# Other banks for one pair of output blocks, later landings for a batch's first loads, and a new instruction order in a fused attention and FFN kernel

## The chip, the cores and the metric

The kernel runs on one core of a Trainium2 chip. The metric is the device time of one execution in microseconds (us); the median of a few executions is compared.

The core's engines run side by side, each through its own list of instructions in a fixed order, and wait for each other by semaphores: PE (TensorE) multiplies matrices, DVE (VectorE) and ACT (ScalarE) work elementwise, POOL (GpSimd) here casts and issues DMAs, and SP (SyncE) issues DMAs. Sixteen DMA engines move the data. PE writes its results to PSUM, which has eight banks; DVE and ACT read them from there.

## The reference

Clustered attention for 4 batches, 8 heads, 768 positions and 64 dimensions, and then a gated FFN over the 3072 positions with 512 features and 1536 hidden units:

```
q_assign = argmax(q_n · c_n)            # 16 centroids per head, normalised; k_assign in the same way
scores   = where(q_assign == k_assign, scale * q·kT, -1e9)
attn     = exp(scores - max) / sum
x        = (attn · v), heads side by side
out      = (sigmoid(x @ w_gate) * (x @ w_val)) @ w_out
```

## The kernel before, in words

**Tiling.** Heads are taken in pairs (`p`, four of them per batch). Positions are split in even and odd halves; a group `(b, gr)` is the half `gr` of batch `b`, 384 positions (in batch 0: 256 and 512). A block is one head pair in one group.

**Attention.** `load_nat` (L444) loads k and q of a head pair into a buffer `nat`. For batch 0 and for the first half of batch 1's pairs, PE transposes them (L617, L795, L903) into a `ring` bank; for the rest DVE does (L595). Copies go to `t32`, POOL casts to `even` (L650), a DMA on SP shifts half of it to `odd` (L654). PE multiplies with the centroids (L687, L835, L948), DVE makes one-hot rows of the best cluster (L549, L556, L563, L574), and DMAs put these rows below the features (L334), so that the score matmul with 80 rows gives the mask as well. `attend` (L983) then does, for two units at a time: two score matmuls into an `sc` buffer (L1008), one exponential on ACT into `es` (L1032), and the value matmuls into the `av` bank (L1059). At the end of a block DVE divides (L1084, L1089), and a transposing DMA on SP (L1117), or PE (L1097), puts the result into `x`.

**FFN.** `feed` (L1409) runs for a group when its attention is done. For a hidden chunk of 128 it makes a gate and a value projection into two `ring` banks (L1422, four matmuls each), a tanh on ACT (L1585), and a product on DVE into `hT` (L1596). Pairs of chunks that stand in `seven` are made with seven instead of eight products (L1498), whose sums go through ACT copies (L1517) and DVE additions (L1529, L1544); in the last group, (3, 1), both of the first banks of these seven products are one `sc` buffer, and elsewhere two `ring` banks. `project` (L1187) multiplies two blocks of 128 positions with w_out, again with seven products (L1275, six matmuls each), sums on DVE (L1244, L1306, L1310, L1327, L1331, L1348) and one ACT copy (L1321). Its argument `many` decides where its results and sums stand: with `many` in two `sc` buffers and in three buffers `late` (batch loads' buffers, free by then), else in two `ring` banks and in buffers `s22`, `s11`, `s12`, `half`, `diff`.

**PSUM.** The eight banks are two `sc` buffers of two banks, one `av` bank and three `ring` banks.

**What sets the order.** No order is written by hand. Each step is added to a list (`od.add`) with an engine, a cost, its dependencies, a due time, a latency `lat` behind its end, and the buffers it takes. `Order.schedule` (L129) goes through a model of time: of the steps that could start first on an engine it takes the one with the smallest due time. What it finds is the order of instructions on each engine; the due times come from `due_at` for attention slots and `due_ffn` for FFN work. So a changed constant moves instructions on all engines, and nothing else. A POOL or SP DMA may wait for an older one of its queue.

Of the kernel before, what the change touches and what calls it, by code (L numbers as in the profile page):

```python
# [209 lines left out]
def kernel(  # L210
# [108 lines left out]
    def due_at(slot):  # L319
        return T1 + (slot - S1) * (0.403 if slot < S1 else 0.826)  # L320

# [122 lines left out]
    def load_nat(b, p, nm, eng, due, early=0.0, hold=None, behind=()):  # L444
# [38 lines left out]
        if hold:  # L483
# [12 lines left out]
                1.05, held, due, acq=[] if held else [buf], uses=[buf] if held else [], early=early,  # L496
                seq=behind, lat=2.0 if b else (0.2 if p == 1 else 1.0),
            )
# [80 lines left out]
    def prepare(b, grp, due, step, act=(), queues=("SP",), split=False):  # L579
# [116 lines left out]
        for half in range(2):  # L696
# [33 lines left out]
            if split or half:  # L730
                n_ = 0
                cs = cols if split else ALL
                for e in range(2):
                    for pos, p in enumerate(grp):
                        for g, nm in ((2 * pos, "k"), (2 * pos + 1, "q")):
                            r = 32 * g + 16 * e
                            m = dma(
                                queues[n_ % len(queues)],
                                lambda p=p, e=e, nm=nm, cs=cs: aug[b, p][e].tile[64:80, NM[nm], cs],
                                lambda r=r, cs=cs: oht.tile[r : r + 16, cs],  # L740
                                0.04 if split else 0.07,

                                [a5, shifted[b, p, half]], due - (20.0 if (b, grp[0]) == (1, 0) else 0),
                                uses=[oht, aug[b, p][e]], lat=3.2,
                            )
                            n_ += 1
                            for h in (half,) if split else (0, 1):
                                masked[b, p, e, nm, h].append(m)
# [30 lines left out]
    def prepare_pair(b, p, due, step, act=("q",), direct=False):  # L779
# [82 lines left out]
        if direct:  # L862
            place(
                b, p, oh, tiles, last, due + (3.0 if p == 1 else 0.0), [c["k", 0], c["k", 1]],
                {(nm, e, h): c[nm, e] for nm in ("k", "q") for e in range(2) for h in range(2)},
            )
            return
# [115 lines left out]
    def attend(block, at, slot):  # L983
# [15 lines left out]
        for i, (e, j) in enumerate(some):  # L999
            kb = aug[b, p][j % 2]  # L1000

            def score(i=i, e=e, j=j, kb=kb):
# [15 lines left out]
                    masked[b, p, j % 2, "k", e] + masked[b, p, par, "q", e],  # L1018
                    due - (33.5 if early else 0.0), lat=0.25,
                    acq=[] if i else [sc], uses=[kb, qb_] + ([sc] if i else []),  # L1020
# [32 lines left out]
        def value():  # L1053
# [14 lines left out]
            value, [t2] + [vload[b, p][e] for e in dict.fromkeys(e for e, _ in some)],  # L1068
            due + (-4.1 if last else 5.5) - (19.5 if early else 0.0), lat=0.25 if last else 0.0,
            seq=exps[-1:], acq=[av] if first else [], uses=[es] + ([] if first else [av]),  # L1070
# [116 lines left out]
    def project(b, one, two, final, many, end):  # L1187
# [45 lines left out]
        def add(to, place, x, y, op, behind=(), on="DVE"):  # L1233
            tasks = []
            on = "DVE" if end else on
            for n, (i0, i1) in enumerate(parts):
# [11 lines left out]
                        (done1 if done1 is not done2 else []) + done2[: 2 * i1] + list(behind)[n : n + 1],  # L1248
                        due - -13.0 - (6.0 if end and not n else 0.0), lat=0.13, acq=fresh, both=True,
                        uses=hs + [buf for buf in to if buf not in fresh],  # L1250
# [158 lines left out]
    def feed(b, gr, work):  # L1409
# [23 lines left out]
        free = [h_last[hs_[-3]]] if len(hs_) > 2 else []  # L1433
        seven = WP[: {(0, 0): 0, (0, 1): 0, (1, 0): 2, (1, 1): 2, (2, 0): 2, (2, 1): 3, (3, 0): 3, (3, 1): 2}[b, gr]]
        if not wsums_of:
            for n, fa in enumerate(WP):
                sum_up_weights(n, fa, 70.0 + 2 * n)
# [11 lines left out]
        if seven:  # L1449
            for n, (to, x, y) in enumerate(  # L1450
# [6 lines left out]
                def differ(to=to, x=x, y=y, n=n):  # L1457
                    if not n:
# [4 lines left out]
                    od.add(  # L1463
                        "DVE", 0.28, differ, xdone[b, gr] + t_tasks[-1:], due_ffn(work) - 6.0, lat=0.12, both=True,
                        acq=[] if n else [tb], uses=[xb] + ([tb] if n else []), seq=free,
# [3 lines left out]
        def seven_products(fa, work):  # L1469
# [39 lines left out]
            def copied(i, r_, m, eng="ACT", y=0):  # L1509
# [3 lines left out]
                def go():  # L1513
# [7 lines left out]
                return od.add(  # L1521
                    eng, 0.375 if eng == "ACT" else 0.47, go, [m], due_ffn(work) - 5.0, lat=0.16,
                    acq=[to] if new else [], uses=[r_] + ([] if new else [to]),
# [93 lines left out]
        if len(blocks_of) % 2:  # L1617
# [3 lines left out]
        pairs = [  # L1621
            project(b, blocks_of[i], blocks_of[i + 1], end and i + 2 == len(blocks_of), (end and i > 0) or (b, gr) == (B - 1, 0), end)
            for i in range(0, len(blocks_of), 2)
# [22 lines left out]
    load_v(0, NP - 1, "SP", -7.7 + p_, 20.0 + 4.5 * NP, behind=nat[0, NP - 2, "v"])  # L1646
    WT = (12.5, 16.0, 23.0, 24.0, 29.5, 29.5, 38.0, 29.0, 43.0)
    n = 0
# [15 lines left out]
    for block in blocks:  # L1664
        b, gr, p, part = block
        if (gr, p) == (0, 0) and b + 1 < B:
            for grp in ((0, 1), (2, 3)):
                due = due_at(first_slot(b + 1, grp[0]))
                for p_ in grp:
                    for nm in ("k", "q"):  # L1670

                        load_nat(
                            b + 1, p_, nm, "POOL" if (b, grp[0]) == (0, 2) else "SP", max(due - 45.0, 20),
                            due - 60 if b else 40.0 if grp[0] else 14.5,
                        )
                prepare(b + 1, grp, max(due - 27.5, 45.5) + (9.0 if (b, grp[0]) == (0, 2) else 0), 1.31)
        at = 0
# [5 lines left out]
        if done[b, gr] == NP * len(groups[b, gr]):  # L1683
            if b + 1 < B:
                for p_ in (2 * gr, 2 * gr + 1):
                    due = due_at(first_slot(b + 1, p_))
                    load_v(b + 1, p_, "POOL", due - 32.0, due - 15, due - 12.5)
            work = feed(b, gr, work)
# [45 lines left out]
```

## Time and profile before

| what | value |
|---|---|
| median of 3 runs | 315.62 us (315.27 to 318.08) |
| the profiled execution's own time | 316.29 us |
| its span, first to last instruction | 314.5 us |
| PE, DVE, ACT, POOL busy | 97%, 75%, 75%, 25% |
| matmuls on PE | 3251 |
| granted TensorE clock, mean | 0.999 |
| HBM read, written | 28.34 MB, 6.29 MB |

How to read it: in the lists of instructions the first number is the start in us from the beginning of the span, then the time taken, the engine, the line of the kernel, the operation, what it writes <- reads, shapes, a count, and in brackets the idle time of the engine before it with what ended that. A matmul's row spans its way through the array, so that rows of matmuls overlap: the cost of one is read from start to start. Rows with SPq or a POOL DMA are the issue of a transfer, not its landing.

### The profile page before, as it was taken

To read this page: it belongs to the slowest core of one execution; us is meant where nothing else is said; L and a number is where in the kernel's file an instruction comes from. 1 tells how busy PE (TensorE), PEld (TensorE's weight loads), DVE (VectorE), ACT (ScalarE), POOL (GpSimd) and SP (SyncE) were. 2 spreads that over 40 slices of the span, in tenths; PEclk is the share of its full clock that TensorE was granted. 3 is DMA by queue.
4 is the path that set the end of the run, shared out by engine and by line. 5 is a ranking of instruction groups with operands and counts; after the bars stand their busy time and mean duration, and the time that the engine had idled before them with its cause. 6 is when DMAs were issued, how large, how long until landed. Compare 5 with 4: busy or idle time off the path is not lost.

```text
span 314.5 us, 8301 instructions
## 1 busy us (share of the span) xinstructions
PE 303.7 (97%) x3251; PEld 223.0 (71%) x3251; DVE 236.5 (75%) x575; ACT 235.0 (75%) x365; POOL 77.5 (25%) x110
## 2 busy tenths in 40 slices
PE   7998899999999999999999999999999999999895
PEld 3677688644578867757776877757777888768674
DVE  4999847799978749885486978977475944786893
ACT  4799899332999979868897768957899778943521
POOL 5897563881011401340002200470000000000000
PEclk9999999999999999999999999999999999999999
DMA  6999999994465886891465683996200022000003
GB/s 216 376 273 150 238 215 121 124 147 68 82 101 105 142 137 176 105 113 40 106 102 88 104 185 94 100 122 59 83 6 15 15 81 79 16 2 36 34 0 133
DMA packets 97430, 34.49 MB, mean 110 GB/s; under 512 B 83136, under 2 KB 93296, under 8 KB 97392
## 3 DMA queue, kind: packets, MB, share of 16 engines
q1 hardware_dynamic: 72048, 24.30, 34.1%
q0 software_dynamic: 24336, 8.65, 27.1%
q10 hardware_dynamic: 1008, 1.02, 0.9%
q8 instruction: 25, 0.41, 0.5%
q14 instruction: 13, 0.11, 0.1%
HBM read 28.34 MB, written 6.29 MB: 110 GB/s over the span
## 4 chain that ended last, share of the span: by engine, by line
PE 83%; ACT 5%; DMA 5%; DVE 5%; issue 1%; DVEq 0%; SPq 0%; ACTq 0%
PE ring L1422 28%; PE sc L1008 17%; PE ring L1275 15%; PE av L1059 9%; PE ring L1498 8%; ACT es L1032 3%; PE sc L687 3%; DMA nat<-in_q_dram 3%; PE sc L1275 2%; DMA out_dram<-out 1%; PE sc L1498 1%; DMA cn<-in_centroids_dram 1%; DVE t L577 1%; DVE even L574 1%; ACT nat L1517 1%
## 5 line engine op out<-in xcount | busy, mean ns | idle before, releaser
L1032 ACT ACTIVATE es<-sc,nbias 128x768 f16<-128x768 f32 (+1 forms) x189 | 168.6, 923 | 18.4 <-PE sc L1008 17.0
L1059 PEld LDWEIGHTS <-es 128*128 128x128 f16 x1152 | 54.9, 97 | 15.0 <-issue 0.2
L1059 PE MATMUL av<-vp,es 128*128 128x65 f16 x1152 | 60.1, 193 | 0.0
L1585 ACT ACTIVATE gt<-ring 128x384 f32<-128x384 f32 (+2 forms) x68 | 34.2, 503 | 33.9 <-PE ring L1422 26.2
L1422 PE MATMUL ring<-x,wv 128*128 128x384 f16 (+2 forms) x272 | 55.3, 325 | 0.1
L1422 PE MATMUL ring<-x,wg 128*128 128x384 f16 (+2 forms) x272 | 55.4, 326 | 0.0
L1596 DVE SCALAR_TENSOR_TENSOR hT<-gt,ring 128x384 f16<-128x384 f32 (+2 forms) x68 | 37.2, 548 | 21.7 <-PE ring L1422 18.1
L650 POOL CAST even<-t 128x768 f16<-128x768 f32 x24 | 20.5, 871 | 118.8 <-DVE t L595 59.7
L1422 PEld LDWEIGHTS <-wv 128*128 128x128 f16 x272 | 25.0, 97 | 15.8 <-issue 0.8
L1422 PEld LDWEIGHTS <-wg 128*128 128x128 f16 x272 | 24.6, 98 | 15.9 <-issue 2.5
L1275 PEld LDWEIGHTS <-hT 128*128 128x128 f16 x294 | 27.1, 98 | 4.6
L1008 PE MATMUL sc<-even 80*128 80x384 f16 (+2 forms) x120 | 26.3, 293 | 1.7 <-ACT es L1032 1.2
L1008 PE MATMUL sc<-odd,even 80*128 80x384 f16 x96 | 26.3, 326 | 0.4 <-ACT es L1032 0.4
L1008 PE MATMUL sc<-odd 80*128 80x384 f16 x96 | 26.4, 325 | 0.1
L1008 PE MATMUL sc<-even,odd 80*128 80x384 f16 (+2 forms) x120 | 26.4, 293 | 0.1
L1008 PEld LDWEIGHTS <-even 80*128 80x128 f16 x216 | 19.9, 98 | 7.5 <-issue 1.6
L1008 PEld LDWEIGHTS <-odd 80*128 80x128 f16 x216 | 19.5, 98 | 7.6 <-issue 2.9
L1529 DVE TENSOR_TENSOR nat<-ring,nat 128x384 f32<-128x384 f32 x26 | 13.9, 551 | 10.1 <-ACT nat L1517 8.6
L1498 PEld LDWEIGHTS <-wss 128*128 128x128 f16 x224 | 19.0, 97 | 3.5 <-issue 1.9
L595 DVE STREAM_TRANSPOSE t<-nat 128x384 f32<-128x384 f32 x40 | 21.4, 556 | 0.0
L334 POOL DMA_DIRECT2D vp<-in_v_dram x24 | 19.7, 833 | 0.1
L1089 DVE TENSOR_TENSOR xn<-av,rr 128x384 f16<-128x384 f32 (+2 forms) x36 | 18.2, 506 | 0.8
(140 smaller groups left out, 456.3 us busy)
## 6 DMA issues: line engine op xcount, KB each, us to landing
out_dram<-out SPq DMA_DIRECT2D x21, 256.0 KB, 2.4
nat<-in_k_dram SPq DMA_DIRECT2D x32, 96.0 KB, 3.0
nat<-in_q_dram SPq DMA_DIRECT2D x32, 96.0 KB, 3.0
odd<-even SPq DMA_DIRECT2D x12, 192.0 KB, 3.2
vp<-in_v_dram POOLq DMA_DIRECT2D x24, 96.0 KB, 4.8
nat<-in_k_dram SPq DMA_DIRECT2D x5, 384.0 KB, 6.9
nat<-in_q_dram SPq DMA_DIRECT2D x5, 384.0 KB, 7.2
nat<-in_v_dram SPq DMA_DIRECT2D x4, 384.0 KB, 6.9
```

Source lines behind the costliest of these rows:

```text
L334: eng, (0.74 if eng == "POOL" else 0.69) if pkt == 13 else ISSUE[eng], lambda: Q[eng].dma_start(out=out_of(), in_=in_of()),
L595: nc.vector.transpose(t[:, half * QB : (half + 1) * QB].rearrange("p (c x) -> p c x", x=128), blocks_[:, half],)
L650: nc.gpsimd.tensor_copy(t[:, NM[nm], cols], t32[p, nm].tile[:, cols])
L1008: nc.tensor.matmul(out=to, lhsT=kb.tile[0:80, 0, e * QB + j // 2 * 128 : e * QB + (j // 2 + 1) * 128], rhs=qb_.tile[0:80, 1, e * QB + c0 * ...
L1032: i = nc.scalar.activation(to, of, AF.Exp, bias=nbias, scale=D ** -0.5 if quarters(b, p) else scale,).ins
L1059: nc.tensor.matmul(out=av.tile[:, g : g + D + 1], lhsT=es.tile[:, i * N + c * 128 : i * N + (c + 1) * 128], rhs=vp[:, e, j, :], start=firs ...
L1089: nc.vector.tensor_tensor(take(xn)[:, :nq].rearrange("p c (e d) -> p (c e) d", d=D), sums()[:, :, 0:D], rr.tile[:, : 2 * nq].unsqueeze(2). ...
L1275: nc.tensor.matmul(out=ps[:, lo:hi], lhsT=left_()[:, i], rhs=right(i)[:, n0 : n0 + w], start=new and i == 0, stop=i == NFC // 2 - 1, skip_ ...
L1422: nc.tensor.matmul(out=ps[:, :N], lhsT=ws[fc // FPG][:, dcc, fc % FPG, :], rhs=xb.tile[:, dcc, :N], start=(dcc == 0), stop=(dcc == NDC - 1),)
L1498: nc.tensor.matmul(out=ps[:, f], lhsT=w_[:, d, f], rhs=x_()[:, d], start=new and not (f or d), stop=d == 1, skip_group_check=True,)
L1585: lambda rg=rg, gt=gt: nc.scalar.activation(take(gt)[:, :N], rg.tile[:, :N], AF.Tanh, scale=0.5),
L1596: nc.vector.scalar_tensor_tensor(t[:, fc, :N], gt.tile[:, :N], 1.0, rv.tile[:, :N], ALU.add, ALU.mult)
```

## The change

The last pair of group (3, 0) no longer asks for `many`; `seven` of the last group is written out as chunk pairs 2 and 4 (the dictionary gave the first two of `WP`, which are 2 and 4); the planner's latency for loads of whole `nat` buffers of later batches (in effect those of the first two head pairs of batch 1) goes from 2.0 to 3.0; and constants of due times, early times and latencies are set anew. `WT` holds the due times of the weights' loads in order of issue. Nothing else in the code differs.

```diff
     def due_at(slot):
-        return T1 + (slot - S1) * (0.403 if slot < S1 else 0.826)
+        return T1 + (slot - S1) * (0.386 if slot < S1 else 0.826)
...
# load_nat, a whole buffer
-                seq=behind, lat=2.0 if b else (0.2 if p == 1 else 1.0),
+                seq=behind, lat=3.0 if b else (0.2 if p == 1 else 1.0),
...
# prepare, the DMA of a one-hot row
-                                uses=[oht, aug[b, p][e]], lat=3.2,
+                                uses=[oht, aug[b, p][e]], lat=2.7,
...
# prepare_pair, direct
-                b, p, oh, tiles, last, due + (3.0 if p == 1 else 0.0), [c["k", 0], c["k", 1]],
+                b, p, oh, tiles, last, due + (4.0 if p == 1 else 0.0), [c["k", 0], c["k", 1]],
...
# attend, scores
-                    due - (33.5 if early else 0.0), lat=0.25,
+                    due - (29.5 if early else 0.0), lat=0.25,
...
# attend, values
-            due + (-4.1 if last else 5.5) - (19.5 if early else 0.0), lat=0.25 if last else 0.0,
+            due + (-8.1 if last else 5.5) - (19.5 if early else 0.0), lat=0.25 if last else 0.0,
...
# project, sums of hT
-                        due - -13.0 - (6.0 if end and not n else 0.0), lat=0.13, acq=fresh, both=True,
+                        due - -14.0 - (6.0 if end and not n else 0.0), lat=0.13, acq=fresh, both=True,
...
# feed
         seven = WP[: {(0, 0): 0, (0, 1): 0, (1, 0): 2, (1, 1): 2, (2, 0): 2, (2, 1): 3, (3, 0): 3, (3, 1): 2}[b, gr]]
+        if (b, gr) == (B - 1, 1):
+            seven = (2, 4)
...
-                        "DVE", 0.28, differ, xdone[b, gr] + t_tasks[-1:], due_ffn(work) - 6.0, lat=0.12, both=True,
+                        "DVE", 0.28, differ, xdone[b, gr] + t_tasks[-1:], due_ffn(work) - 5.0, lat=0.12, both=True,
...
-                    eng, 0.375 if eng == "ACT" else 0.47, go, [m], due_ffn(work) - 5.0, lat=0.16,
+                    eng, 0.375 if eng == "ACT" else 0.47, go, [m], due_ffn(work) - 3.0, lat=0.16,
...
-            project(b, blocks_of[i], blocks_of[i + 1], end and i + 2 == len(blocks_of), (end and i > 0) or (b, gr) == (B - 1, 0), end)
+            project(b, blocks_of[i], blocks_of[i + 1], end and i + 2 == len(blocks_of), end and i > 0, end)
...
-    WT = (12.5, 16.0, 23.0, 24.0, 29.5, 29.5, 38.0, 29.0, 43.0)
+    WT = (14.5, 16.0, 23.0, 24.0, 29.5, 29.5, 38.0, 29.0, 42.5)
...
-                            b + 1, p_, nm, "POOL" if (b, grp[0]) == (0, 2) else "SP", max(due - 45.0, 20),
-                            due - 60 if b else 40.0 if grp[0] else 14.5,
+                            b + 1, p_, nm, "POOL" if (b, grp[0]) == (0, 2) else "SP", max(due - 45.5, 20),
+                            due - 60 if b else 37.5 if grp[0] else 14.5,
...
-                prepare(b + 1, grp, max(due - 27.5, 45.5) + (9.0 if (b, grp[0]) == (0, 2) else 0), 1.31)
+                prepare(b + 1, grp, max(due - 27.5, 45.5) + (9.0 if (b, grp[0]) == (0, 2) else 0), 1.37)
...
-                    load_v(b + 1, p_, "POOL", due - 32.0, due - 15, due - 12.5)
+                    load_v(b + 1, p_, "POOL", due - 32.0, due - 15, due - 13.5)
```

## The prediction

> **What bounds the kernel now.** I read the page first (span, busy shares), then the busy time by windows, then the waits of PE, and then the order in time on PE, SP, ACT and DVE around each wait. The shares:
>
> ```profile
> span 314.5 us, 8301 instructions
> PE 303.7 (97%) x3251; PEld 223.0 (71%) x3251; DVE 236.5 (75%) x575; ACT 235.0 (75%) x365; POOL 77.5 (25%) x110
> ```
>
> In the windows the columns are the stretch, its length, and the busy time of PE, PEld, DVE, ACT and POOL, then the clock, the busy share of the DMA engines (over 1 where packets overlap) and GB/s.
>
> ```profile
> 30.00:40.00 10.00, 8.10 (x120) 6.61 (x117) 8.59 (x24) 8.76 (x11) 5.23 (x7) 1.00 1.21 229
> 50.00:270.00 220.00, 219.82 (x2360) 159.68 (x2358) 167.20 (x383) 174.36 (x271) 42.37 (x53) 1.00 0.61 95
> 290.00:300.00 10.00, 9.20 (x75) 6.54 (x74) 7.74 (x19) 5.23 (x13) 0.00 (x0) 1.00 0.15 54
> ```
>
> From 50 to 270 us PE is idle for 0.18 us: nothing can be won there, and any new wait there is paid in full. What can be won lies before 50 us, where ACT is as full as PE, and behind 270 us. The waits of PE name the two places:
>
> ```profile
> PE ring L617 <- DMA nat<-in_q_dram: 1.2, 1, 1.2
> PE sc L1498 <- DVE nat L1529: 0.5, 1, 0.5
> PE sc L1498 <- ACT p L1517: 0.3, 1, 0.3
> ```
>
> The clock is 1.00 in every window, so no term below needs it.
>
> **Part 1: what changes nothing by itself.** `seven = (2, 4)` for the last group equals what the dictionary gave (two of WP = two, four): 0 us. PE issues the same matmuls before and after, and DVE, ACT, POOL and SP the same counts of work. So the change is order and banks, and PE's sum of work stays; the time moves only by idle time of PE that goes or comes.
>
> **Part 2: batch 1's first loads.** The larger `lat` (2.0 to 3.0) makes the planner expect these loads later. In the new order the two transposes of `nat` for k of head pair 0 stand side by side instead of two score groups apart, and the load of q for head pair 1, which takes over their buffer, is issued on SP ahead of two transposing DMAs and one row copy instead of behind them. The old order on PE and SP, and the landing (from the chain that ended last):
>
> ```profile
> 23.98 0.52 PE L617 MATMUL ring<-ident,nat 128*128 128x128 f32 x3
> 33.77 0.49 PE L1008 MATMUL sc<-odd,even 80*128 80x384 f16 x2
> 35.41 0.52 PE L617 MATMUL ring<-ident,nat 128*128 128x128 f32 x3 [1.15 <-DMA nat<-in_q_dram]
> ```
> ```profile
> 19.31 0.61 SPq L334 DMA_DIRECT2D odd<-even  x1
> 23.43 1.20 SPq L1117 DMA_TRANSPOSE x<-xn  x1
> 24.71 0.54 SPq L334 DMA_DIRECT2D odd<-even  x1
> 25.54 1.15 SPq L1117 DMA_TRANSPOSE x<-xn  x1
> 26.79 1.44 SPq L334 DMA_DIRECT2D nat<-in_q_dram  x1
> ```
> ```profile
> 26.79 8.49 DMA nat<-in_q_dram
> ...
> 281.69 1.31 PE sc L1275 x12
> ```
> ```profile
> 36.30 4.52 ACT L1032 ACTIVATE es<-sc,nbias 128x768 f16<-128x768 f32 x5 [1.10 <-PE sc L1008]
> ```
>
> The buffer is free by 24.50 in the old order (the second transpose starts at 23.98 and takes 0.52), but SP reaches the load only at 26.79: 2.3 us are lost to the queue. In the new order the buffer is free about 1.5 to 2 us sooner, I estimate at 22.5, and nothing stands before the load on SP behind the row copy of 19.31. With the same 8.49 us it lands at 31.0; PE comes to it at 34.10 (33.77 and two matmuls of 0.16). Even issued only at 24.5 it would land at 33.0. So the wait goes. PE lost 35.41 - 34.10 = 1.31 us by starts, but ACT, which paces this stretch, was idle 1.10 us for it (the row of 36.30): I take 1.1. Bounds: 0, if the load lands as late as before, and 1.3. What comes after it is next late is ACT itself, full from 36.30 on.
>
> What is moved behind the load on SP: two transposing DMAs and a row copy, each 1.44 us later at most by the load's issue. The projections that read them stand behind the transposes of 35.41 in PE's order: cost 0 by that cover, and if it were gone, at most the 1.4 us. POOL issues the first gate weights three casts later; they are read behind the same place: 0.
>
> [...]
>
> **Part 3: the tail.** The pair of blocks of group (3, 0) that is multiplied with w_out beside the start of group (3, 1)'s FFN took both `sc` banks; now it takes two of the three `ring` banks, and the `s22`, `s11`, `s12`, `half`, `diff` buffers. The seven products of (3, 1) live in `sc` and had to wait until the pair was read out. The old rows, in order of time:
>
> ```profile
> 280.23 0.81 PE L1422 MATMUL ring<-x,wg 128*128 128x384 f16 x4
> 280.50 0.55 DVE L1596 SCALAR_TENSOR_TENSOR hT<-gt,ring 128x384 f16<-128x384 f32 x1
> 280.88 0.81 PE L1422 MATMUL ring<-x,wv 128*128 128x384 f16 x4
> ...
> 289.31 0.48 ACT L1517 COPY p<-sc 128x384 f32<-128x384 f32 x1
> ...
> 290.50 0.49 PE L1498 MATMUL sc<-x,wg 128*128 128x192 f16 x4
> ...
> 290.83 0.49 PE L1498 MATMUL sc<-nat,wss 128*128 128x192 f16 x4
> ...
> 291.22 0.56 DVE L1529 TENSOR_TENSOR nat<-sc,nat 128x384 f32<-128x384 f32 x1 [1.21 <-ACT nat L1517]
> 291.83 0.49 PE L1498 MATMUL sc<-nat,wss 128*128 128x192 f16 x4 [0.50 <-DVE nat L1529]
> ...
> 301.58 0.60 PE L1275 MATMUL ring<-wo,hT 128*128 128x256 f16 x4
> ```
>
> By starts, a projection (P, 4 matmuls) takes 0.65 (280.23 to 280.88), a seven-product step (Q) 0.33 (290.50 to 290.83), a w_out product (J, 6 matmuls) 0.65 (1.31 for twelve in the chain's row of 281.69, quoted above). From 280.23 to the first product of the last pairs at 301.58, 21.35 us, the order holds 16 P, 14 Q and 7 J: 10.4 + 4.6 + 4.6 = 19.6 us. So 1.75 us are waits. One is seen whole: 290.83 to 291.83 is 1.00 us for a Q of 0.33. They come from one chain: both sevens can begin only behind the old pair, then run through ACT and DVE with little else between.
>
> In the new order the first Q stands behind four P, the seven J of the pair lie between the steps of the first seven, and the second seven follows. I went through it by hand from 280.23 with the rows' durations: a reader starts 0.27 us behind the start of the next group (280.23 to 280.50), a DVE instruction takes 0.55, an ACT copy 0.48, PE restarts 0.05 behind them (291.78 to 291.83). First Q 282.83; J 283.16 to 285.13; two Q; four J 285.78 to 288.40; four Q to 289.72; then PE waits about 0.4, since DVE must first do the pair's two mixes and last sum and then the Q's own sum: next Q at 290.15; from there P and Q alternate without a wait, and the last P ends at 300.25. That is 1.33 us before 301.58: I take -1.3. Bounds: -1.75, all waits gone, and +0.5, if the single free ring bank makes as many half-us waits as it removes and one more; -1.3 is nearer the first since every other step found its bank free.
>
> Cover of this: six of the ring uses in that stretch are J on the two held banks; P, which needs all three, stands before and behind. If the held banks were read later than about 289.5, the P behind would wait for them one to one.
>
> **Part 4: the rest of the order.** Score and sum due times move by up to 4 us; the row copies of the one-hots are expected 0.5 us sooner (`lat` 3.2 to 2.7). Inside 50 to 270 us the new order differs by neighbours that change place. Cost 0, with PE's 0.18 us of idle time as the row; bounds 0 and +0.5, one wait like the largest of the tail. The last block of w_out's first third (`wo0`) moves on POOL from ahead of batch 1's later loads to behind them, beside its last third; its sums, four DVE instructions, move later, into a stretch in which DVE is full:
>
> ```profile
> 60.00:80.00 20.00, 20.00 (x113) 9.26 (x112) 19.29 (x43) 7.44 (x13) 9.17 (x12) 1.00 0.89 113
> ```
>
> In exchange three others move out behind it, so I take 0 for the difference of one.
>
> **The sum.** -1.1 - 1.3 + 0 = -2.4 us. The profiled execution took 316.29 us (span 314.5 and 1.8 around it): 313.9 for such a one. The median shown, 315.62, is 0.67 below it, so I predict 313.2 against that median.
>
> **The rivals.**
> (a) The load does not land sooner, since the DMA engines are full: the wait at 35.41 stays, and only the tail is won: 314.3. For it: the share of 1.21. Against: loads of this kind and size land a like time behind their issue, 7.2 us in the median of five, so landing follows issue:
>
> ```profile
> nat<-in_q_dram SPq DMA_DIRECT2D x5, 384.0 KB, 7.2
> ```
>
> Chance 0.10.
> (b) The tail's gain is eaten, since the pair holds two of three ring banks: 314.5, the first term alone. For it: three banks fed P without a wait, one can't. Against: the hand count. The Trainium skill (Perfetto Trace Analysis, "Optimization Strategy") says that a gap repeating on the engine that should be full can mean too little PSUM for the next tile; by it this rival is what a shared bank gives. Chance 0.12.
> (c) Slower. DVE's in-order wait for batch 1's last q quarters: POOL now issues `wo0` and the last third back to back ahead of them.
>
> ```profile
> 72.69 1.03 DVE L595 STREAM_TRANSPOSE t<-nat 128x384 f32<-128x384 f32 x2
> ```
> ```profile
> 62.07 3.09 POOL L334 DMA_DIRECT2D nat<-in_q_dram  x4 [1.36 <-DVE t L595]
> ```
> ```profile
> wo<-in_moe_w_out_dram POOLq DMA_DIRECT2D x3, 512.0 KB, 10.6
> nat<-in_q_dram POOLq DMA_DIRECT2D x8, 96.0 KB, 4.4
> ```
>
> Behind this DVE row stand the reads that free ring banks, so PE stops some 1.7 us (one P pair at 512 columns, an estimate from 0.65 per 384) after DVE does. The fourth quarter is issued at about 64.4 and lands 4.4 us later, at 68.8; DVE comes to it at 72.69, or 71.6 with the first term won. If `wo0` adds its whole 10.6 us, it lands at 79.4, DVE is 7.8 us late, PE 6.1: 315.62 - 2.4 + 6.1 = 319.3. Up to 2.8 us of delay it costs nothing, from 6.9 on the kernel is slower than before. Against: the loads ahead of them start sooner by what `wo0` took before, so the queue as a whole is not longer. Chance 0.08.
> (d) It does nothing that counts, both terms given back by new waits in between: 315.6. Chance 0.06.
> (e) More goes: all 1.75 in the tail, 1.3 early, and 0.4 of the other 0.75 us that PE is idle from 30 to 40 us: 312.2. Chance 0.09.
>
> **How the numbers follow.** The forecast has 0.55, with its own range 312.3 to 314.2 (half of each term's doubt). 1% is 3.2 us, about what a measurement of this kernel can tell from no change: faster by over 1% is below 312.46, held by (e) and the lower edge of the forecast: 0.18. Slower by over 1% is above 318.8: (c) at its full price, 0.07. The rest, 0.75, is within 1%. The range 311.8 to 316.2 leaves out (c), and parts of (e).
>
> **What would show it.** Right: the PE wait on in_q_dram at L617 is gone; ACT's idle 1.10 us near 36 is gone; the first run of L687 (batch 1's second half) starts 1.1 us sooner; the first L1498 on `sc` of the last group stands about 3 us behind its first L1422, and the waits of L1498 shrink from 0.8 to about 0.4; the last products start 1.3 us sooner after the first P. Wrong: PE waits at L1422 behind the pair's ring banks near 289 to 292; DVE waits at L595 between 68 and 75; a wait over 0.5 us between 50 and 270. A span above 314 would say that a term failed.

## The result, and the profile after

The changed kernel takes 313.38 us in the median of six runs (312.99 to 313.82), the kernel before 316.36 beside it (315.27 to 318.08): a ratio of 0.9904, 95% interval 0.9884 to 0.9924. That is 3.0 us or 0.96% less. Its profiled execution took 313.21 us, with a span of 311.4 against 314.5: 3.1 us less in the trace, where the prediction had 2.4.

The page of the kernel after; the count of matmuls is that of before (3251) and the busy time of PE the same within 0.1 us (303.8, before 303.7), so all of it is idle time of PE that went:

```profile
span 311.4 us, 8300 instructions
...
PE 303.8 (98%) x3251; PEld 223.1 (72%) x3251; DVE 236.6 (76%) x575; ACT 234.7 (75%) x365; POOL 77.2 (25%) x110
```

Its busy time by windows (columns as in the prediction), and its waits of PE:

```profile
20.00:30.00 10.00, 9.44 (x130) 7.36 (x129) 9.31 (x26) 9.61 (x13) 9.03 (x13) 1.00 1.12 194
30.00:40.00 10.00, 9.50 (x143) 8.22 (x141) 8.85 (x26) 10.00 (x14) 6.76 (x9) 1.00 1.24 209
...
50.00:270.00 220.00, 220.00 (x2363) 159.19 (x2362) 167.55 (x380) 174.29 (x270) 42.21 (x52) 1.00 0.60 97
...
290.00:300.00 10.00, 9.99 (x70) 6.57 (x69) 8.97 (x25) 4.05 (x9) 0.00 (x0) 1.00 0.01 2
```
```profile
PE sc L1008 <- ACT es L1032: 0.9, 2, 0.5
...
PE sc L1500 <- DVE nat L1531: 0.5, 1, 0.5
```

From 30 to 40 us PE is busy for 9.50 us instead of 8.10, from 290 to 300 for 9.99 instead of 9.20, and in the middle for all 220.00 instead of 219.82. The wait for `in_q_dram` at L617 is gone. (From L1437 on, line numbers are two higher than before: L1500 is the old L1498.)

Three places date the gain. The first product of L687, before and after:

```profile
57.85 1.50 PE L687 MATMUL sc<-t,cblk 128*32 128x384 f32 x16
```
```profile
55.85 1.50 PE L687 MATMUL sc<-t,cblk 128*32 128x384 f32 x16
```

The first P (L1422) of the last group starts at 280.23 before, the first product of the last pairs at 301.58; after, they stand here:

```profile
278.01 0.81 PE L1422 MATMUL ring<-x,wg 128*128 128x384 f16 x4
...
280.61 0.49 PE L1500 MATMUL sc<-x,wg 128*128 128x192 f16 x4
280.94 0.82 PE L1275 MATMUL ring<-wo,hT 128*128 128x256 f16 x6
...
287.18 0.49 PE L1500 MATMUL sc<-nat,wss 128*128 128x192 f16 x4
288.17 0.49 PE L1500 MATMUL sc<-nat,wss 128*128 128x192 f16 x4 [0.50 <-DVE nat L1531]
...
298.50 0.82 PE L1275 MATMUL ring<-wo,hT 128*128 128x256 f16 x6
```

So 2.22 us are won ahead of the tail (280.23 to 278.01), 2.00 of them ahead of 58 us, and 0.86 in the tail (a stretch of 21.35 us, now 20.49). The early gain is twice what was predicted, the tail's two thirds.

On SP the load of q is issued at 22.70 us, ahead of two transposing DMAs and a row copy, and lands 5.03 us later:

```profile
19.30 0.61 SPq L334 DMA_DIRECT2D odd<-even  x1
22.70 0.39 SPq L334 DMA_DIRECT2D nat<-in_q_dram  x1
24.27 1.21 SPq L1117 DMA_TRANSPOSE x<-xn  x1
25.57 0.54 SPq L334 DMA_DIRECT2D odd<-even  x1
26.52 3.27 SPq L1117 DMA_TRANSPOSE x<-xn  x2
```

and ACT, idle for 1.10 us at 36.30 before, runs through:

```profile
29.49 8.74 ACT L1032 ACTIVATE es<-sc,nbias 128x1024 f16<-128x1024 f32 x10 [0.32 <-PE sc L1008]
```

### The profile page after: what moved, and what is told of

Same layout as the page of the kernel before. It is cut to its first block, busy times and chain, and to the rows that moved or that the text cites. A ratio compares the mean times of both kernels' runs of the same rounds, so it can differ in the third digit from the quotient of the medians.

```text
span 311.4 us, 8300 instructions
## 1 busy us (share of the span) xinstructions
PE 303.8 (98%) x3251; PEld 223.1 (72%) x3251; DVE 236.6 (76%) x575; ACT 234.7 (75%) x365; POOL 77.2 (25%) x110
## 4 chain that ended last, share of the span: by engine, by line
PE 92%; ACT 4%; DVE 1%; DMA 1%; issue 0%; SPq 0%; ACTq 0%
PE ring L1422 29%; PE sc L1008 19%; PE ring L1275 16%; PE av L1059 11%; PE ring L1500 9%; ACT es L1032 3%; PE sc L687 3%; PE sc L1275 1%; PE sc L1500 1%; DMA nat<-in_k_dram 1%; PE ring L795 1%; PE ring L617 1%; PE ring L835 1%; PE ring L903 0%; PE ring L948 0%
## 5 line engine op out<-in xcount | busy, mean ns | idle before, releaser
L1059 PEld LDWEIGHTS <-es 128*128 128x128 f16 x1152 | 53.9, 97 | 14.0
L1059 PE MATMUL av<-vp,es 128*128 128x65 f16 x1152 | 59.0, 194 | 0.0
L1422 PE MATMUL ring<-x,wv 128*128 128x384 f16 (+2 forms) x272 | 55.4, 326 | 0.1
L1422 PE MATMUL ring<-x,wg 128*128 128x384 f16 (+2 forms) x272 | 55.3, 326 | 0.0
L1598 DVE SCALAR_TENSOR_TENSOR hT<-gt,ring 128x384 f16<-128x384 f32 (+2 forms) x68 | 37.1, 547 | 19.7 <-PE ring L1422 16.0
L1422 PEld LDWEIGHTS <-wv 128*128 128x128 f16 x272 | 24.8, 97 | 16.7 <-issue 2.1
L1422 PEld LDWEIGHTS <-wg 128*128 128x128 f16 x272 | 24.4, 97 | 14.8 <-issue 1.0
L595 DVE STREAM_TRANSPOSE t<-nat 128x384 f32<-128x384 f32 x40 | 21.3, 555 | 2.0 <-DMA nat<-in_q_dram 1.7
L1500 PEld LDWEIGHTS <-wss 128*128 128x128 f16 x224 | 19.1, 97 | 2.7 <-issue 0.6
L1275 PEld LDWEIGHTS <-s 128*128 128x128 f16 x198 | 18.4, 97 | 3.1 <-DVE s L1244 0.2
```

Of the source, the lines that this page charges most:

```text
L595: nc.vector.transpose(t[:, half * QB : (half + 1) * QB].rearrange("p (c x) -> p c x", x=128), blocks_[:, half],)
L1059: nc.tensor.matmul(out=av.tile[:, g : g + D + 1], lhsT=es.tile[:, i * N + c * 128 : i * N + (c + 1) * 128], rhs=vp[:, e, j, :], start=firs ...
L1275: nc.tensor.matmul(out=ps[:, lo:hi], lhsT=left_()[:, i], rhs=right(i)[:, n0 : n0 + w], start=new and i == 0, stop=i == NFC // 2 - 1, skip_ ...
L1422: nc.tensor.matmul(out=ps[:, :N], lhsT=ws[fc // FPG][:, dcc, fc % FPG, :], rhs=xb.tile[:, dcc, :N], start=(dcc == 0), stop=(dcc == NDC - 1),)
L1500: nc.tensor.matmul(out=ps[:, f], lhsT=w_[:, d, f], rhs=x_()[:, d], start=new and not (f or d), stop=d == 1, skip_group_check=True,)
L1598: nc.vector.scalar_tensor_tensor(t[:, fc, :N], gt.tile[:, :N], 1.0, rv.tile[:, :N], ALU.add, ALU.mult)
```

## The experiments

The planner rebuilds the whole order for any changed constant. So most kernels below leave the constants alone and move single steps in the finished order, ahead of the writing out of instructions; all other instructions keep their place. They share these two edits, and each has its own `mended`:

```diff
-        order = self.schedule()
+        order = mended(self.schedule(), self.moved)
         for t in order:
...
-    od.run()
+    od.moved = nat[1, 1, "q"][0]; od.run()
```

Milestones of all kernels from their traces, in us. "L687" is the first product of batch 1's second half; "tail" is the stretch from the first P of the last group to the first product of the last pairs; the load is that of q for head pair 1 of batch 1. Each ratio is to the kernel before as measured beside that kernel (medians of 315.98 to 316.38 us).

| kernel | load issued, landed | L687 | tail | median time | ratio to before (95%) |
|---|---|---|---|---|---|
| before | 26.79, 35.28 | 57.85 | 21.35 | 316.36 | |
| after | 22.70, 27.73 | 55.85 | 20.49 | 313.38 | 0.9904 (0.9884 to 0.9924) |
| e1, before with the banks | 26.75, 34.85 | 57.42 | 20.49 | 315.27 | 0.9963 (0.9942 to 0.9983) |
| e2, after without the banks | 23.08, 27.57 | 56.17 | 21.35 | 313.92 | 0.9914 (0.9886 to 0.9942) |
| e3, before with the load ahead | 24.74, 29.02 | 56.55 | 21.35 | 315.11 | 0.9954 (0.9937 to 0.9972) |
| e4, after with the load behind | 28.61, 35.82 | 57.81 | 20.49 | 316.48 | 1.0006 (0.9980 to 1.0033) |
| e5, before with both moves | 24.72, 30.15 | 56.51 | 20.50 | 314.04 | 0.9935 (0.9919 to 0.9951) |
| e6, before with three due times | 22.73, 29.26 | 56.36 | 21.36 | 315.22 | 0.9973 (0.9957 to 0.9988) |
| e7, after, two P ahead | 22.71, 27.84 | 55.79 | 20.50 | 313.06 | 0.9904 (0.9888 to 0.9920) |
| e8, after, last q late | 23.03, 28.33 | 56.11 | 20.50 | 314.80 | 0.9955 (0.9938 to 0.9971) |
| e9, before, weights late | 28.52, 32.99 | 63.56 | 21.34 | 320.52 | 1.0132 (1.0108 to 1.0156) |
| e10, after, one P ahead | 22.66, 28.42 | 55.76 | 20.24 | 312.90 | 0.9887 (0.9865 to 0.9908) |
| e11, before, latency alone | 27.07, 35.53 | 58.01 | 21.35 | 316.31 | 1.0010 (0.9990 to 1.0029) |

Kernels with the same early order differ by up to 0.4 us at L687 from one profile to the next (before and e1; after, e2, e7 and e8); the tail's stretch repeats to 0.01 or 0.02, and PE's idle time from 20 to 40 us is 1.06 to 1.08 in all five with the changed early order and no wait for the load (after, e2, e7, e8 and e10). (One expectation, that of e10, counts the stretch from one P earlier; its 21.14 us is 20.49 here.)

**e1 and e2: the banks alone, and the rest without them.**

```diff
# e1, on the kernel before
-project(..., (end and i > 0) or (b, gr) == (B - 1, 0), end)
+project(..., end and i > 0, end)
# e2 puts the old argument back into the changed kernel
```

> The kernel before with the third part of the change alone: the last pair of group (3, 0) takes two ring banks and the buffers s22, s11, s12, half and diff; all constants as before. The order of instructions then differs from that of the kernel before in the tail alone. Theory T (the banks of the pair set the tail): the stretch from the first projection (P) of the last group to the first product of the last pairs shrinks from 21.35 us to about 20.5, the value of the changed kernel, so 0.9 us less, 315.5 us against 316.4; nothing moves ahead of 270 us. Rival B (the tail's gain comes from the moved due times, and the ring banks eat what the pair gives): 21.3 us in that stretch and 316.4. My hand count of 20.02 us would be 315.1.

> The changed kernel with its third part undone: the last pair of group (3, 0) stands in both score buffers again; all constants as changed. Theory T: the stretch from the first P of the last group to the first product of the last pairs goes from 20.5 us back to about 21.35, the time from 313.4 to about 314.3 us, and the early gain of some 2.2 us stays. Rival B: the stretch stays at 20.5 us and the time at 313.4.

Both ends of the stretch, in e1 and then in e2:

```profile
279.80 0.81 PE L1422 MATMUL ring<-x,wg 128*128 128x384 f16 x4
...
300.29 0.82 PE L1275 MATMUL ring<-wo,hT 128*128 128x256 f16 x6
```
```profile
278.40 0.81 PE L1422 MATMUL ring<-x,wg 128*128 128x384 f16 x4
...
299.75 0.82 PE L1275 MATMUL ring<-wo,hT 128*128 128x256 f16 x6
```

The stretch is 20.49 and 21.35 us: the banks are worth 0.86 us with the old constants and with the new, and none of the tail's gain comes from a moved due time. Rival (b) is out. The medians (1.0 less in e1, 0.5 more than the changed kernel in e2) agree within their intervals.

**e3 and e4: one load moved on SP alone.**

```diff
# e3, on the kernel before: right behind the last reader of the buffer
+def mended(order, load):
+    order.remove(load)
+    free = max(order.index(u) for u in load.acq[0].before.users)
+    order.insert(free + 1, load)
+    return order
# e4, on the changed kernel: behind the third DMA of SP that follows it
+    sp = [t for t in order if t.eng == "SP"]
+    third = sp[sp.index(load) + 3]
+    order.remove(load)
+    order.insert(order.index(third) + 1, load)
```

> The kernel before with one instruction moved on one queue: the load of q for head pair 1 of batch 1 is issued on SP right behind the transposes that free its buffer, ahead of one row copy and one transposing DMA. PE, ACT, DVE and POOL keep the order of before, instruction by instruction. Theory Q (what the early part wins is the place of that load on SP): it is issued at about 24.6 us and lands between 29.6 (5.0 us later, as in the changed kernel) and 33.1 (8.5 us later, as before), ahead of 34.1 when PE comes to it; the wait of 1.15 us at L617 is gone and the first product of the last group starts 1.1 to 1.3 us sooner: 315.2 us against 316.4. Theory O (the early gain of 2.2 us is the order of PE's and ACT's instructions as well): the same 1.1 to 1.3 us here, and the other 1.0 us does not come. Rival A (the transfer engines are full, the load lands at 35.3 wherever it is issued): 316.4 us and the wait stays.

> The changed kernel with that load alone put back on SP behind two transposing DMAs and a row copy; the other engines keep the changed order. Theory Q: it is issued at about 28 us and lands between 33.0 (5.0 us later) and 36.5 (8.5 us later); PE comes to it at 33.97, so the kernel loses between 0 and 2.2 us, about 1.1 by the middle: 314.5 us. Rival A (the landing does not follow the issue): 313.4 us, no wait at L617. Theory O: at most the 1.3 us of the old wait come back, and 0.9 us of the early gain stay.

SP's queue in e3, and PE's two transposes of that load:

```profile
23.44 1.20 SPq L1117 DMA_TRANSPOSE x<-xn  x1
24.74 0.53 SPq L334 DMA_DIRECT2D nat<-in_q_dram  x1
25.37 0.52 SPq L334 DMA_DIRECT2D odd<-even  x1
```
```profile
34.11 0.49 PE L617 MATMUL ring<-ident,nat 128*128 128x128 f32 x3
34.77 0.49 PE L617 MATMUL ring<-ident,nat 128*128 128x128 f32 x3
```

The wait is gone (34.11 where before stood 35.41), L687 starts 1.30 us sooner and the median falls by 1.2 us: the forecast's -1.1 for this step, by this step. In e4 the same load behind the same kinds of DMA brings the wait back, larger than it was:

```profile
28.61 0.61 SPq L334 DMA_DIRECT2D nat<-in_q_dram  x1
```
```profile
35.95 0.52 PE L617 MATMUL ring<-ident,nat 128*128 128x128 f32 x3 [1.62 <-DMA nat<-in_q_dram]
```

In the new order the transposing DMAs ahead of it start later on SP, so the load goes out at 28.61 instead of 26.79. That costs 1.96 us at L687 against the changed kernel (1.64 against e2), and 2.1 us by the profiled executions' own times (315.28 and 313.21); the median rises by 3.1, since e4's times scatter (last section). In the new order the place of this one DMA decides whether the change is worth anything.

**e5: both moves, no constant changed.** The edits are those of e1 and e3 together.

> The kernel before with both parts and nothing else: the ring banks for the last pair of group (3, 0), and the load of q moved ahead on SP. No constant of a due time or latency is changed. If the parts are independent, 1.2 us (load alone) and 0.9 us (banks alone, from the tail's stretch) add up: 316.3 - 2.1 = 314.2 us; first L687 at 56.5 us, the tail's stretch 20.5 us. Theory O (the new order brings a further 0.5 to 0.8 us ahead of 50 us): the changed kernel stays ahead of this one by that. Theory Q alone (the load and the banks are all): 313.4 us, as the changed kernel.

314.04 us: the two parts add up (316.0 for the kernel before beside it, less 1.2 and 0.9, is 313.9), and the changed kernel stays 0.66 us ahead. e7 below, measured beside e5, has the changed kernel's early order and a tail of the same 20.50 us, and takes 313.06: 1.0 less. So there is a third part of 0.7 to 1.0 us, which the new order brings. In windows, e5's PE is as idle as that of e3 from 20 to 40 us; e5's rows:

```profile
20.00:30.00 10.00, 9.09 (x136) 7.21 (x134) 9.36 (x26) 9.65 (x12) 9.53 (x14) 1.00 1.17 218
30.00:40.00 10.00, 9.37 (x144) 7.97 (x141) 9.11 (x26) 9.85 (x13) 6.35 (x9) 1.00 1.25 206
...
50.00:270.00 220.00, 219.83 (x2351) 159.53 (x2349) 167.29 (x382) 174.22 (x270) 42.69 (x53) 1.00 0.59 95
```

PE is idle for 1.54 us from 20 to 40 here and 1.06 in the changed kernel, 0.17 from 50 to 270 and 0.00 there: 0.65 together, about the size of what is left.

**e6 and e11: which constant moves the load.**

```diff
# e6, on the kernel before: the change's due times of attention slots, of the one-hots' placing and of the weights
-        return T1 + (slot - S1) * (0.403 if slot < S1 else 0.826)
+        return T1 + (slot - S1) * (0.386 if slot < S1 else 0.826)
-                b, p, oh, tiles, last, due + (3.0 if p == 1 else 0.0), [c["k", 0], c["k", 1]],
+                b, p, oh, tiles, last, due + (4.0 if p == 1 else 0.0), [c["k", 0], c["k", 1]],
-    WT = (12.5, 16.0, 23.0, 24.0, 29.5, 29.5, 38.0, 29.0, 43.0)
+    WT = (14.5, 16.0, 23.0, 24.0, 29.5, 29.5, 38.0, 29.0, 42.5)
# e11, on the kernel before
-                seq=behind, lat=2.0 if b else (0.2 if p == 1 else 1.0),
+                seq=behind, lat=3.0 if b else (0.2 if p == 1 else 1.0),
```

> The kernel before with three of the changed constants: the slope of the due times (0.403 to 0.386), the due time of the one-hot's placing for head pair 1 (3.0 to 4.0), and the due times of the first and last weight loads. The latency stays 2.0. The planner then puts the load of q ahead on SP by itself, and the first 208 matmuls' steps stand as in the changed kernel. Theory O: the early part comes out as in the changed kernel, first L687 at 55.9 to 56.2 us against 57.4 to 57.9 before, with no wait at L617 on the load; the latency of 3.0, to which the prediction put it, has no part in it. Rival: the latency is needed, and the first L687 stands at 57.4 or later. The time has the old tail, and whatever the middle of this order costs: 314.5 us if that is nothing.

> The kernel before with the planner's latency of those loads alone changed from 2.0 to 3.0, to which the prediction put the move of the load on SP. In the order that the planner then writes out, the load stands on SP where it stood, behind two transposing DMAs and a row copy, and PE's transposes of it stand about one score step later. If the latency were what brings the early gain, 315.2 us and no wait at L617 on the load. If it is the load's place on SP (and the latency does not move it there), the load is issued at about 26.8 us and lands at about 35 as before, PE comes to it some 0.2 us later than before, a wait of about 1 us stays, and the time is 316.3 us, give or take 0.5 for the order of the rest.

In e11 the load is issued at 27.07 and PE still waits for it, 0.6 us where about 1 was expected:

```profile
PE ring L617 <- DMA nat<-in_q_dram: 0.6, 1, 0.6
```

Its time is that of before (1.0010, 0.9990 to 1.0029). The latency alone does not move the load, and with 2.0 in the changed kernel's text the planner writes out the very same order. e6 has the old latency, and its load goes out at 22.73 without a wait at L617:

```profile
20.00:30.00 10.00, 9.29 (x122) 7.21 (x121) 9.14 (x26) 10.00 (x13) 8.96 (x13) 1.00 1.21 174
30.00:40.00 10.00, 9.58 (x152) 8.15 (x149) 9.20 (x26) 9.68 (x13) 6.49 (x9) 1.00 1.23 214
...
50.00:270.00 220.00, 219.70 (x2348) 158.97 (x2347) 167.86 (x381) 173.78 (x270) 43.11 (x54) 1.00 0.60 95
```

PE's idle time from 20 to 40 us falls to 1.13, close to the changed kernel's 1.06. So the due times bring the load's place and the smaller early idle time. But L687 came at 56.36, a little later than expected and 0.19 before e3's, and the middle gives 0.12 us back (219.70). The time, 0.8 us under before, is 0.7 above the expected 314.5 and no better than that of e3 (315.22 and 315.11): what the smaller idle time is worth in this kernel is not shown.

**e7 and e10: the wait left in the tail.**

```diff
# e7, on the changed kernel; -31 and -29 are P, -36 and -30 steps of the sevens, counted from PE's last task
+    pe = [t for t in order if t.eng == "PE"]
+    for late, ahead_of in ((-31, -36), (-29, -30)):
+        order.remove(pe[late])
+        order.insert(order.index(pe[ahead_of]), pe[late])
# e10 moves -31 ahead of -36 alone
```

> The changed kernel with two projections of the last group moved ahead on PE, each in front of one step of the seven products: the one that starts at 289.81 goes in front of the step that waits at 288.17, the one at 290.79 in front of the step at 290.46. Nothing else moves; both banks are free by 287.4. Theory W (the wait of 0.66 us at 288.17 is PE standing behind the readers of one bank, with other work at hand): the wait is filled, the products of the last pairs start 0.3 to 0.7 us sooner, 312.9 us against 313.4. Rival: the chain of readers (ACT copy, DVE sum) sets the pace, the next steps wait instead, and the time stays at 313.4.

> The changed kernel with one projection of the last group moved ahead on PE, in front of the step that waits at 288.17; the second one stays where it was. When both were moved, the wait of 0.66 us came back at 292.00, as the next step's inputs were 0.13 us sooner only. Theory C (the chain step, ACT copy, DVE sum, step sets the pace, and a projection between two of its steps costs only what it delays them): the step at 290.46 starts at about 290.1, the one at 292.14 at about 291.8, and the products of the last pairs 0.3 to 0.4 us sooner, 313.0 us against 313.4. Rival (something behind it, the release of ring banks, sets the pace): the stretch from the first P to the last pairs stays at 21.14 us, counted from the P behind the last transposes, and the time at 313.4.

In e7 the wait at 288.17 is filled and another of the same size comes up at 292.00; in e10 it shrinks:

```profile
290.33 0.49 PE L1500 MATMUL sc<-nat,wss 128*128 128x192 f16 x4
...
292.00 0.49 PE L1500 MATMUL sc<-nat,wv 128*128 128x192 f16 x4 [0.53 <-DVE p L1531]
```
```profile
290.04 0.49 PE L1500 MATMUL sc<-nat,wss 128*128 128x192 f16 x4 [0.24 <-ACT nat L1519]
...
291.70 0.49 PE L1500 MATMUL sc<-nat,wv 128*128 128x192 f16 x4
...
298.07 0.82 PE L1275 MATMUL ring<-wo,hT 128*128 128x256 f16 x6
```

The stretch is 20.50 us in e7 (nothing won) and 20.24 in e10 (0.25 won). From the first to the second of the steps shown it takes 1.67 us in e7 and 1.66 in e10 (1.68 in the changed kernel, 290.46 to 292.14), whatever stands between them. In e7 the second P stood in front of the first of these steps and delayed it, and with it the chain of step, ACT copy, DVE sum, next step; the work that filled one gap was missing in the next. The chain sets the pace, as e10's theory has it, but the gain is 0.25, not 0.3 to 0.4. e10 is the fastest kernel, 312.90 us; its 0.5 us under the changed kernel is within the intervals, and what its trace shows is 0.25.

**e8: the slower rival, tried.**

```diff
# on the changed kernel: the four quarters behind the next three loads of v and three casts
+    pool = [t for t in order if t.eng == "POOL"]
+    for i in range(62, 66):
+        order.remove(pool[i])
+        order.insert(order.index(pool[71]) + 1 + i - 62, pool[i])
```

> The changed kernel with the prediction's slower rival made on purpose: the four quarters of the last q of batch 1 are issued on POOL behind the next three loads of v and three casts, at 66.9 to 69.9 us instead of 59.2 to 62.3. They land at about 74.4 us instead of 67.3, 3.7 us after DVE comes to them at 70.69. By the prediction's price (PE stops 1.7 us after DVE does) PE loses 2.0 us: 315.4 us, with a wait of DVE at L595. Rival: DVE's wait is taken up by the slack of its later work, and the time stays within 0.5 us of 313.4.

The quarters land sooner than expected (median 3.8 us behind their issue), so DVE waits for 2.24 us:

```profile
73.27 1.04 DVE L595 STREAM_TRANSPOSE t<-nat 128x384 f32<-128x384 f32 x2 [2.24 <-DMA nat<-in_q_dram]
```

PE stops in the middle of the sixteen products that read these transposes:

```profile
73.91 1.48 PE L687 MATMUL sc<-t,cblk 128*32 128x384 f32 x10 [0.29 <-DVE t L595]
75.31 1.04 PE L1422 MATMUL ring<-x,wg 128*128 128x512 f16 x4
```

From the first of these products (72.77) to the P behind them it takes 2.54 us, against 1.43 in e2 (72.83 to 74.26): most of the loss is made here. The last transposes by PE (L1097) start at 278.64 us, against 277.36 in e2, whose early part runs alike (L687 at 56.11 and 56.17): 1.28 us of DVE's 2.24 reach PE, and 1.4 us the median. DVE's wait is where the rival had it. What PE stands for is another thing than the prediction said: the transposes themselves, not the reads behind them that free ring banks; and PE is covered for about 1.0 us, not 1.7.

**e9: why the load lands sooner.** Moving it in e3 put it ahead of a row copy and a transposing DMA on SP, and ahead of POOL's weight loads as well, which begin at 25.3 us. e9 takes only the latter away.

```diff
# on the kernel before
+    pool = [t for t in order if t.eng == "POOL"]
+    wg1, wv1, wo1, wg2, wv2 = [t for t in pool if t.dma][2:7]
+    casts = [t for t in pool[pool.index(wv2):] if not t.dma][:4]
+    for t, cast in ((wg1, 0), (wv1, 1), (wg2, 2), (wo1, 3), (wv2, 3)):
+        order.remove(t)
+        order.insert(order.index(casts[cast]) + 1, t)
```

> The kernel before with the five weight loads of 512 KB that POOL issues from 25.3 to 29.0 us put behind the next four casts, at about 32 to 39 us; SP keeps its order, so the load of q is issued at 26.8 us as before, behind the same transposing DMAs and row copies. It tells apart what made that load land 8.1 to 8.5 us behind its issue in the old place and 4.3 to 5.4 us in the new one. Theory S (it shares the DMA engines with POOL's weight loads): it now lands about 5 us behind its issue, at 31 to 32.5, ahead of 34.1, and the wait of 1.15 us at L617 is gone, without any move on SP. Theory Q2 (it waits on SP's own queue behind the transposing DMAs): it lands at 34 to 35 as before and the wait stays. The time is 315.1 us by S and 316.2 by Q2, if the weights are still in time: the first one is read at 46.1 us.

The whole execution begins some 1.7 us later here, so the load goes out at 28.52; it stands in its old place on SP. The DMA issues from 20 to 36 us, of before and of e9 (KB of one, us from issue to landing):

```profile
nat<-in_q_dram SPq DMA_DIRECT2D x1, 384.0 KB, 8.5
```
```profile
nat<-in_q_dram SPq DMA_DIRECT2D x1, 384.0 KB, 4.5
```

8.5 us became 4.5 with nothing changed on SP, and the wait at L617 is gone: theory S. What made the load slow was sharing the DMA engines with 512 KB loads of another queue. The price shows what those loads covered. DVE's sums of the weights wait for them in order, and PE waits behind DVE:

```profile
43.99 0.42 DVE L1403 TENSOR_TENSOR wss<-wv 128x512 f16<-128x512 f16 x1 [4.23 <-DMA wv<-in_moe_w_val_dram]
```
```profile
47.30 0.53 PE L1059 MATMUL av<-vp,es 128*128 128x65 f16 x12 [3.48 <-DVE xn L1089]
```

So the kernel is 4.1 us slower. I had counted from PE's first read of the weights (46.1 us before) and overlooked DVE's sums of them, which come first.

## Why the prediction was right, and where it was not

The total was near: -2.4 us by the prediction, -3.0 measured, a time of 313.2 against 313.38. That the times agree better than the differences is luck: the kernel before came out at 316.36 beside the changed one, and the forecast was made from 315.62. The sum comes out otherwise than it was made: load -1.2 (predicted -1.1), tail -0.9 (-1.3), order -0.7 to -1.0 (0). The errors of the last two have opposite signs, so the total is better than its terms; that is luck as well.

**Part 1** (nothing by itself): right; the same matmuls and busy time.

**Part 2** (the load of q): the mechanism and the size hold, by e3 and e4, and rival (a) fails, though half of what it says is true. The engines are shared, and it is the reason for the old 8.49 us (e9). The Trainium skill (DMA: Bandwidth & Descriptors, "Queues, rings and completion order") says that each DMA engine takes turns between the queues that have work; e9 agrees, with 4.5 us without POOL's weight loads beside it and 8.5 with them. What doesn't follow is that the load lands no sooner: ahead of the burst the load lands in 4.3 to 6.5 us (e3 and e6), and those 2 to 4 us come on top of the earlier issue. The prediction kept 8.49 for the new place and still had the wait gone. Its step on the code failed: the larger latency does not move the load (e11), the due times do (e6). I had read the latency's purpose into the new order, and hadn't taken the constants one by one.

**Part 3** (the tail): right in kind, -0.86 instead of -1.33. The hand count is exact up to the last step ahead of the wait: it has the first step of the sevens 2.60 us behind the first P and the fourth step's end 9.49 behind it; the trace has 2.60 (280.61 - 278.01) and 9.50. The step that failed is the wait behind it, about 0.4 counted (290.15 less 289.72) and 0.66 measured (288.17, less 287.18 and 0.33), and 0.24 more behind that, where I had counted P and Q "without a wait". Of these, 0.18 stand at one P, which starts at 293.29, 0.83 behind the P before it instead of 0.65, and 0.05 behind the end of DVE's product (L1598) of 292.69. The reason given for the wait was wrong too. I named DVE's mixes and last sum of the pair; but DVE was free and stood idle for ACT's copy, which reads a step of 286.52. The rows of ACT and of DVE:

```profile
287.05 0.48 ACT L1519 COPY nat<-sc 128x384 f32<-128x384 f32 x1 [1.37 <-PE sc L1500]
```
```profile
286.68 0.69 DVE L1348 SCALAR_TENSOR_TENSOR out<-ring,diff 128x512 f32<-128x512 f32 x1
287.56 0.56 DVE L1531 TENSOR_TENSOR nat<-sc,nat 128x384 f32<-128x384 f32 x1 [0.19 <-ACT nat L1519]
```

Rival (b) fails: no P waited for a bank of the pair near 289 to 292.

**Part 4** (the rest of the order at 0, bounds 0 and +0.5): wrong in sign. It brings 0.7 to 1.0 us (e5 against the changed kernel and e7); 0.5 of it shows as idle time of PE from 20 to 40 us and 0.2 in the middle. The bound below should have been the idle time that was left there: rival (e) allowed 0.4 of it. Which of the moved instructions brings it was not taken apart, and the cause stays open; e6 has nearly all of the smaller early idle time (1.13 us) with three due times, but not the time.

**Rival (c)** did not come: the load of `wo0` landed at 60.48 us, and DVE came to the quarters at 70.69, 3.4 us behind their landing at 67.28. e8 shows what would have come of it: DVE waits at L595 as the rival says, and PE, covered for 1.0 us, waits for the transposes. **Rival (d)** is out, and **(e)** was near for the early part (1.7 us, 2.2 measured) and wrong for the tail.

Of the signs named ahead all but one held: the L617 wait and ACT's idle time gone, the first step of the sevens 2.6 us behind the first P (3 predicted), the waits of L1498 down from 0.8 to 0.5, no wait of PE from 50 to 270. The one that did not is the tail's: the last products start 0.86 us sooner after the first P, not 1.3. L687 came 2.0 us sooner instead of 1.1, which pointed at once to the part that was missing.

## What to carry to other kernels

A load's place in its queue decides twice: when it is issued, and whose transfers it shares the engines with; ahead of a burst of large loads it landed in 4.3 to 6.5 us here instead of 8.1 to 8.5, so look at what the other queues start within the next microseconds. Where a planner sets the order, take the finished order and move one step in it to price a cause: a changed constant moves instructions everywhere at once, and not always the one that it seems meant for. Work moved into a gap of a chain that runs through several engines wins only as far as the chain's own next steps start sooner: here 0.25 of 0.66 us with one piece of work, and nothing when a second piece delayed the next step.

## What the runs showed of the hardware that was not expected

Where PE waits for this load, times scatter: 314.91 to 318.90 us in the kernel before over all its runs, 315.07 to 318.92 in e4. Without that wait they don't: 314.86 to 315.42 in e3 (ten runs), 312.99 to 313.82 in the changed kernel. So the median gains more than the best run, and taking out a wait for a transfer also takes out its scatter. The cause of the scatter was not tried. Some of the longest runs, not all, show a lower mean clock: 0.987 to 0.995 in six of e4's twelve runs, one of e1's and three of the kernel before, while no run of the changed kernel, e2, e3, e5 to e8 and e10, 59 in all, is below 0.998. e9's profiled run, which has the stretch of low clock shown next, has a mean of 0.995 too. So a part of the scatter may be the clock behind a longer wait; none of these long runs was profiled, so that is not shown.

A gap in PE's work can cost more than its length. In e9, behind the gap of 3.48 us that ends at 47.30, the granted clock (third number from the right) is 0.59 over 4 us:

```profile
43.00:47.00 4.00, 0.82 (x7) 0.46 (x5) 2.94 (x9) 2.14 (x4) 1.74 (x3) 1.00 1.22 229
47.00:51.00 4.00, 3.70 (x32) 2.54 (x32) 1.46 (x5) 1.45 (x3) 1.50 (x2) 0.59 1.24 206
51.00:55.00 4.00, 4.00 (x65) 3.56 (x63) 0.62 (x2) 3.89 (x7) 0.74 (x1) 0.98 1.32 166
```

The Trainium skill (TensorE: Matmul & The Clock Gate, "What's actually happening") says that the clock is halved after an idle window of about 3.4 us and comes back after as long a busy one; these rows agree. The two rows with a lower clock are what about 3.4 us at half clock would give. The price shows at L687 as well: it comes 5.7 us later than before, 1.7 of it by the late beginning, although the wait of 1.15 us at L617 is gone; that leaves about 5.1 us, other small waits included, for a gap of 3.48. The gaps of about 1 us in the kernel before had no such row.
